# Streamed weight blocks on two DMA queues instead of one, with the small work of the loop moved to ScalarE

## The chip, the cores and the metric

The kernel runs on one core of one Trainium2 chip. The metric is the device time of one execution in microseconds (us), from the first instruction to the last. Below, "PE" is TensorE, "ACT" ScalarE, "DVE" VectorE, "POOL" GpSimd and "SP" SyncE, as the profile has them.

## The reference, cut to what matters

The output holds two independent computations side by side: a recurrent attention (A) and a long convolution (B). The change touches the loop of A only. It goes through 64 segments of 32 new tokens, and each segment needs the memory that the one before produced, so that segments cannot overlap freely:

```python
for s in range(n_seg):                               # 64 segments
    h = concatenate([mem, xs], axis=1)               # 8 memory rows + 32 rows of x
    q, k, v = h @ Wq, h @ Wk, h @ Wv                 # each 1024 x 4096, bf16
    p = softmax(where(mask, q @ k.T * scale, -1e9))
    o = (p @ v) @ Wo                                 # 4096 x 1024
    mem = o[:, :M, :]                                # feeds the next segment
    outs.append(o[:, M:, :])
```

The four matrices have 32 MB, 64 blocks of 512 KB. The kernel keeps 46 of them resident and streams the other 18 from HBM again in every segment.

## The kernel before

Eighteen blocks a segment are streamed, into a pool of four buffers. `unit` hands out a block and starts its load; PE reads the block in the order of the program.

```python
STREAM = {("k", 0): (0, 4), ("q", 0): (0, 4), ("k", 1): (0, 4), ("q", 1): (0, 4), ("v", 0): (0, 4), ("v", 1): (0, 4)}
STREAM_O = (0, 3, 5, 8, 11, 13)                      # 12 + 6 = 18 streamed blocks
...
    wst = ctx_w.enter_context(tc.tile_pool(name="a_wst", bufs=4, side="right"))
...
    def unit(key):
        if key in W_res:
            return W_res[key]                        # a resident block
        t_ = wst.tile([128, 2048], BF16, name="wst", tag="w")
        nc.sync.dma_start(out=t_[:], in_=WD[key][:])
        return t_
...
    # quads (projections): each block is read by 4 matmuls of 128x512
            for kc in kcs:
                w = unit((m, t, kc))
                for g in range(4):
                    nc.tensor.matmul(a[32 * g:32 * g + 32, :], lhsT=hT[:, kc, :], rhs=w[:, 512 * g:512 * g + 512], ...)
...
    # oproj (output projection): each block is read by 8 matmuls of 128x256
            for u in us:
                w = unit(("o", u))
                ...
```

The small loads (`pk`, `xt`), the small copies (`put_xt`, `new_kt`) and the five stores at the end of a segment are GpSimd's. In the change below they are the lines with a minus.

Of the kernel before, what the change touches and what calls it, by code (L numbers as in the profile page):

```python
# [175 lines left out]
def part_a(ctx, tc, x, mem0, src, WD, HE, seg_len, out_a, ahead, W_res, rest):  # L176
    nc = tc.nc
    S, Dm = x.shape
    M = mem0.shape[0]
    SL = seg_len  # L180
# [4 lines left out]
    XM = 24  # L185
    XL = SL - XM
    NK = SL + M
# [3 lines left out]
    XTd, PKd, OLd = ahead.XTd, ahead.PKd, ahead.OLd  # L191
# [16 lines left out]
    for g in range(4):  # L208
        p = slice(32 * g, 32 * g + 32)
# [8 lines left out]
    nc.gpsimd.affine_select(out=BDL[:], in_=BDL[:], compare_op=ALU.is_ge, fill=0.0, base=0, pattern=[[-8, 4], [-32, 4]], channel_multiplier=1)  # L218
    nc.gpsimd.affine_select(out=BDL[:], in_=BDL[:], compare_op=ALU.is_ge, fill=0.0, base=7, pattern=[[8, 4], [32, 4]], channel_multiplier=-1)

    def unit(key):
        if key in W_res:
            return W_res[key]
        t_ = wst.tile([128, 2048], BF16, name="wst", tag="w")
        nc.sync.dma_start(out=t_[:], in_=WD[key][:])
        return t_

    hT = const.tile([128, KC, SL], BF16, name="hT")
# [15 lines left out]

    def load_pk(j):
        pk = pers.tile([128, 768], BF16, name="pk", tag="pk")
        nc.gpsimd.dma_start(out=pk[:], in_=PKd[j])
        return pk

    def load_xt(j):  # L250
        xt = work.tile([128, KC, XM], BF16, name="xt", tag="F")
        nc.gpsimd.dma_start(out=xt[:].rearrange("p k r -> p (k r)"), in_=XTd[j])  # L252
        return xt

    def put_xt(xt):
        nc.gpsimd.tensor_copy(out=hT[:, :, 0:XM], in_=xt[:])

    def bc(ap, shape):
        return ap.to_broadcast(shape)

    put_xt(load_xt(0))
    pk = load_pk(0)
    for s in range(NS):
        vl = pk[:, 512:768].rearrange("p (t e) -> p t e", t=2)
        kl, ql = ([pk[:, 256 * t + o:256 * t + o + 128].rearrange("p (a g k) -> p a g k", a=4, g=4) for t in range(2)] for o in (0, 128))

        def quads(m, t, kcs, a=None):
            if a is None:
                a = ps_acc.tile([128, 512], F32, name="acc", tag="acc")
# [3 lines that stand above are left out]
                    nc.tensor.matmul(a[32 * g:32 * g + 32, :], lhsT=hT[:, kc, :], rhs=w[:, 512 * g:512 * g + 512],  # L273
                                     start=(kc == 0), stop=(kc == KC - 1), tile_position=(0, 32 * g), skip_group_check=True)
            return a
# [13 lines left out]

        def new_kt(t):  # L290
            k = work.tile([128, 4, 4, NK], BF16, name="KT", tag="C")
            nc.gpsimd.tensor_copy(out=k[:, :, :, SL:NK], in_=kl[t])  # L292
            return k

        def scores(t, QT, KT):
# [43 lines left out]
        def pv(p, t, V, pb, lbs, first=True):  # L339
            for hl in range(4):  # L340
                nc.tensor.matmul(p[:, hl, :], lhsT=V[:, 128 * hl:128 * hl + 128], rhs=pb[:, hl, :],
                                 start=(first and hl == 0), stop=False, skip_group_check=True)
            n = 4 // len(lbs)
            for i, lb in enumerate(lbs):
                nc.tensor.matmul(p[:, n * i:n * i + n, :].rearrange("p a b -> p (a b)"), lhsT=vl[:, t, :], rhs=lb,  # L345
                                 start=False, stop=True, skip_group_check=True)
# [9 lines left out]
        def evac_o(p, tag):  # L356
            o = work.tile([128, 4, 4, SL], BF16, name="oT", tag=tag)
            nc.scalar.copy(out=o[:], in_=p[:].rearrange("p a (g q) -> p a g q", g=4))  # L358
            return o

        def pv_l(pl_, t, V, L):

            pv(pl_[:, t], t, V, L[:, 0].rearrange("p (a b) k -> p a (b k)", a=4), [L[:, 1].rearrange("p a k -> p (a k)")], first=(t == 0))

        def oproj(po, us, oT):
            for u in us:
                w = unit(("o", u))
                for hh in range(2):
                    h = 2 * u + hh
                    for qt in range(4):  # L370
                        nc.tensor.matmul(po[32 * qt:32 * qt + 32, :], lhsT=oT[:, h % 4, (h % 16) // 4, :],  # L371
                                         rhs=w[:, 1024 * hh + 256 * qt:1024 * hh + 256 * qt + 256],
                                         start=False, stop=(h == 31), tile_position=(0, 32 * qt), skip_group_check=True)
# [4 lines left out]
        a = quads("k", 0, range(KC))  # L378
        k0 = evac(a, "A")
        KT0 = new_kt(0)  # L380
        a = quads("q", 0, range(KC))
        q0 = evac(a, "B")
# [9 lines left out]
        a = quads("q", 1, range(KC))  # L392
        q1 = evac(a, "B")
        KT1 = new_kt(1)
        p1 = new_tr()
        tr(p1, 0, k1, KT1[:, :, :, 0:SL])
# [18 lines left out]
        pp = ps_o.tile([128, 2, 256], F32, name="pp", tag="pp")  # L415
# [3 lines left out]
        if s + 1 < NS:  # L419
            xt = load_xt(s + 1)  # L420
        quads("v", 1, H1, a)
        V1 = evac(a, "E")
        if s + 1 < NS:
            put_xt(xt)
# [7 lines left out]
        pv1 = pv_x(1, V1, pk[:, 0:512].rearrange("p (a b) -> p a b", a=4), [lb1[:].rearrange("p a k -> p (a k)")], "B")  # L432
        o1 = evac_o(pv1, "B")
        pv_l(pl_, 1, V1, L1)
        if s + 1 < NS:
            pk = load_pk(s + 1)
        oproj(pp[:, 1, :], range(8, 16), o1)
        ob = work.tile([128, 2, 256], BF16, name="ob", tag="E")
        osb = ob[:, 0, :]
        nc.vector.tensor_copy(out=osb, in_=pp[:, 1, :])  # L440
        nc.scalar.copy(out=ob[:, 1, :], in_=pp[:, 0, :])
        if s + 1 < NS:
# [1 line left out]
            for j in range(2):  # L444
                nc.tensor.transpose(out=pt_o[:, j, :, :].rearrange("p a b -> p (a b)"), in_=osb[:, 128 * j:128 * j + 128], identity=ident[:])
            nc.vector.tensor_copy(out=hT[:, :, XM:SL].rearrange("p (q j) r -> p j q r", j=2), in_=pt_o[:, :, :, XM:SL])
        nc.gpsimd.dma_start(out=OLd[s], in_=ob[:, 1, :])
        r0 = s * SL
        for qt in range(4):
            nc.gpsimd.dma_start(out=out_a[r0:r0 + XM, 256 * qt:256 * qt + 256], in_=osb[32 * qt:32 * qt + XM, :])  # L450
    ctx_w.close()


    with tc.tile_pool(name="a_eo", bufs=1) as eo, tc.tile_pool(name="a_ew", bufs=16) as ew, \
# [3 lines left out]
        for u in range(16):  # L458
            if u in (0, 2, 4, 6):
# [3 lines left out]
                for n in range(2):  # L463
                    (nc.vector.tensor_copy if n == 0 else nc.scalar.copy)(
                        out=ol[b][:, 16 * n:16 * n + 16, :, :], in_=raw[:, :, 16 * n:16 * n + 16, :].rearrange("p s h k -> p h s k"))
# [13 lines left out]
        for b in range(4):  # L479
            ob = ex_.tile([128, Dm], BF16, name="oel", tag="oel")  # L480
# [586 lines left out]
def kernel(  # L1067
# [42 lines left out]
    with ExitStack() as ctx_a:  # L1110
        part_a(ctx_a, tc, A_x[0], A_mem0[0], src, WD, A_Wo.shape[0] * A_Wo.shape[1], seg_len, out_a, ahead, W_res, rest)
# [35 lines left out]
```

## Time and profile before

| what | before | from |
|---|---|---|
| median time | 2945.86 us (3 runs, 2942.58 to 2952.67) | timed runs |
| loop (first `ob` to last `ob`) | 1026.5 to 2842.2 us, 28.82 us a segment | line of `ob<-pp` |
| moved in the loop | 342 GB/s | busy time by stretch |
| PE waits for streamed blocks | 359 us | tile view |

### The profile page before, as it was taken

The page shows a single profiled execution, that of the slowest core. Times are in us where ns is not written, and L with a number is a line of the kernel's source. Part 1 is how long each engine was busy: PE and PEld are TensorE (multiplying, and loading weights), DVE is VectorE, ACT ScalarE, POOL GpSimd, SP SyncE. Part 2 cuts the span into 40 slices and gives each one's busy share as a digit, 9 for nine tenths or more (in the row PEclk, how much of TensorE's full clock was granted, in tenths as well). Part 3 has the DMA queues.
Part 4 walks back from the last instruction along what each step waited for, and adds up shares of the span by engine and source line. Part 5 has one row for each costly group of instructions (what it writes and reads, how often), then busy time and mean ns, then how long its engine had stood idle before and what let it go on. Part 6 is the DMA issues. An engine that isn't in the chain of part 4 may idle for free.

```text
span 2949.0 us, 75939 instructions
## 1 busy us (share of the span) xinstructions
PE 2124.8 (72%) x32791; PEld 1128.5 (38%) x32838; DVE 1355.8 (46%) x2622; ACT 967.4 (33%) x1394; POOL 599.2 (20%) x993
## 2 busy tenths in 40 slices
PE   1478777846887478777777777777777777777747
PEld 0246444622333244333343333333443333334323
DVE  7577677748983143434333333434333333434320
ACT  4767688731222122222222222222222222222210
POOL 2254435460001111111111111111111111111100
PEclk8689899968899798999899989999899899999978
DMA  4555654534338899999999999999999999999991
GB/s 113 155 156 154 183 164 119 150 115 125 112 128 291 327 348 335 343 338 350 333 352 337 343 332 345 350 345 348 329 336 343 324 353 331 352 339 348 348 322 49
DMA packets 376225, 800.93 MB, mean 272 GB/s; under 512 B 114678, under 2 KB 185334, under 8 KB 373840
## 3 DMA queue, kind: packets, MB, share of 16 engines
q1 hardware_dynamic: 335202, 722.51, 70.8%
q0 software_dynamic: 24912, 51.52, 5.2%
q10 hardware_dynamic: 15774, 22.03, 2.3%
q8 instruction: 257, 4.21, 0.6%
q14 instruction: 80, 0.66, 0.1%
HBM read 742.15 MB, written 67.37 MB: 275 GB/s over the span
## 4 chain that ended last, share of the span: by engine, by line
DMA 43%; PE 20%; issue 20%; DVE 6%; ACT 6%; POOL 5%; SPq 0%; ACTq 0%; POOLq 0%; DVEq 0%
DMA wst<-WD_o 14%; DMA wst<-WD_v 9%; PE acc L273 9%; DMA wst<-WD_k 8%; DMA wst<-WD_q 7%; PE pp L371 2%; PE pe L476 2%; DMA olr<-OLd 1%; ACT sn L859 1%; PE pro L125 1%; POOL us L743 1%; POOL us L744 1%; ACT oT L358 1%; PE tr L284 1%; PE ups L738 1%
## 5 line engine op out<-in xcount | busy, mean ns | idle before, releaser
L273 PEld LDWEIGHTS <-hT 128*32 128x32 bf16 x12288 | 320.7, 100 | 540.1 <-issue 256.7
L273 PE MATMUL acc<-wst,hT 128*32 128x512 bf16 x3072 | 330.2, 415 | 203.2 <-DMA wst<-WD_k 85.2
L279 ACT CAST ev<-acc 128x512 bf16<-128x512 f32 x384 | 225.4, 587 | 528.5 <-PE acc L273 485.8
L371 PEld LDWEIGHTS <-oT 128*32 128x32 bf16 x8192 | 227.8, 102 | 303.3 <-issue 209.8
L371 PE MATMUL pp<-wst,oT 128*32 128x256 bf16 x3072 | 167.0, 296 | 215.8 <-DMA wst<-WD_o 180.7
L285 DVE COPY KT<-tr 128x512 bf16<-128x512 bf16 x128 | 54.4, 425 | 539.8 <-PE tr L284 539.8
L273 PE MATMUL acc<-W_k,hT 128*32 128x512 bf16 x3072 | 249.7, 434 | 0.0
L371 PE MATMUL pp<-W_o,oT 128*32 128x256 bf16 x5120 | 231.5, 294 | 0.0
L273 PE MATMUL acc<-W_q,hT 128*32 128x512 bf16 x3072 | 224.8, 396 | 0.0
L273 PE MATMUL acc<-W_v,hT 128*32 128x512 bf16 x3072 | 212.7, 381 | 0.0
L440 DVE CAST ob<-pp 128x256 bf16<-128x256 f32 x64 | 27.2, 425 | 369.7 <-issue 365.2
L358 ACT CAST oT<-pv 128x512 bf16<-128x512 f32 x128 | 75.3, 588 | 255.7 <-PE pv L345 252.1
L311 DVE TENSOR_REDUCE mx<-sc 128x8 f32<-128x320 f32 x128 | 62.4, 487 | 197.7 <-PE sc L304 197.6
L1033 PE MATMUL yp<-Bt,mi 128*128 128x512 bf16 x379 | 113.8, 405 | 32.3 <-DVE Bt L987 16.3
L951 PE MATMUL hps<-KT,MF 128*128 128x512 bf16 x374 | 100.8, 415 | 49.4 <-DVE x L962 26.1
L252 POOL DMA_DIRECT2D xt<-XTd x64 | 35.9, 561 | 483.9 <-PE pp L345 395.8
L285 ACT COPY QT<-tr 128x512 bf16<-128x512 bf16 x128 | 75.0, 586 | 179.2 <-PE tr L284 141.6
L292 POOL COPY KT<-pk 128x128 bf16<-128x128 bf16 x128 | 38.4, 300 | 462.3 <-PE sc L304 449.4
L450 POOL DMA_DIRECT2D out_dram<-ob x256 | 129.7, 513 | 6.0 <-issue 5.9
L125 PE MATMUL pro<-xTl,wsl 128*128 128x512 bf16 x492 | 113.5, 380 | 8.4 <-DVE ua L740 4.6
L313 ACT ACTIVATE sc<-sc 128x320 f32<-128x320 f32 x128 | 54.0, 422 | 189.0 <-DVE sc L312 157.0
L835 DVE SCALAR_TENSOR_TENSOR nr<-kM,ptt 128x656 f32<-128x656 f32 x128 | 106.1, 829 | 21.5 <-ACT kM L834 18.2
(264 smaller groups left out, 3793.4 us busy)
## 6 DMA issues: line engine op xcount, KB each, us to landing
wst<-WD_o SPq DMA_DIRECT2D x384, 512.0 KB, 5.7
wst<-WD_k SPq DMA_DIRECT2D x256, 512.0 KB, 5.6
wst<-WD_q SPq DMA_DIRECT2D x256, 512.0 KB, 5.3
wst<-WD_v SPq DMA_DIRECT2D x256, 512.0 KB, 5.5
Ud<-ux POOLq DMA_DIRECT2D x16, 1024.0 KB, 5.7
uq<-Ud SPq DMA_DIRECT2D x32, 512.0 KB, 5.5
pk<-PKd POOLq DMA_DIRECT2D x64, 192.0 KB, 5.3
wsl<-in_A_Wk_dram SPq DMA_DIRECT2D x16, 512.0 KB, 4.2
```

Source lines behind the costliest of these rows:

```text
L125: nc.tensor.matmul(a[:], lhsT=w[:, kc, 128 * j:128 * j + 128], rhs=xTl[:, kc, :, :].rearrange("p s k -> p (s k)"), start=(kc == 0), stop=( ...
L273: nc.tensor.matmul(a[32 * g:32 * g + 32, :], lhsT=hT[:, kc, :], rhs=w[:, 512 * g:512 * g + 512], start=(kc == 0), stop=(kc == KC - 1), til ...
L279: nc.scalar.copy(out=q[:], in_=a[:])
L285: eng(out=dst, in_=p[:, i, :, :, :])
L311: nc.vector.tensor_reduce(out=mx[:], in_=sc, axis=AX.X, op=ALU.max)
L358: nc.scalar.copy(out=o[:], in_=p[:].rearrange("p a (g q) -> p a g q", g=4))
L371: nc.tensor.matmul(po[32 * qt:32 * qt + 32, :], lhsT=oT[:, h % 4, (h % 16) // 4, :], rhs=w[:, 1024 * hh + 256 * qt:1024 * hh + 256 * qt + ...
L450: nc.gpsimd.dma_start(out=out_a[r0:r0 + XM, 256 * qt:256 * qt + 256], in_=osb[32 * qt:32 * qt + XM, :])
L476: nc.tensor.matmul(pe[b][n][:], lhsT=ol[b][:, hi, :, :].rearrange("p s k -> p (s k)"), rhs=wos[u][:, 1024 * hh + 512 * n:1024 * hh + 512 * ...
L835: v.scalar_tensor_tensor(out=nrs[e // 4][:, e % 4].rearrange("p f t j -> p f (t j)"), in0=kM[:], scalar=MAGIC, in1=ptv, op0=ALU.subtract, ...
L951: pe.matmul(ps[:], lhsT=MF[:, 4 * rr + mc, cs, 128 * kc:128 * kc + 128], rhs=rhs, start=(i == 0 and mc == 0), stop=(i == 1 and mc == 3))
L1033: pe.matmul(yp[:], lhsT=m_[:, cs, kc, :], rhs=Bt[:, kc, half, j, c_, :], start=(n == 0), stop=(n == 15))
```

## The change

Its intent is to let two DMA queues feed the buffers by turns, so that neither queue has to issue every block. To keep other work from holding up the blocks that GpSimd issues (in the last experiment, where it does, they are issued 5.55 us after their buffer is free), all else that it did in the loop goes to ScalarE.

```diff
+    queues = [nc.gpsimd, nc.sync]
+
     def unit(key):
         if key in W_res:
             return W_res[key]
         t_ = wst.tile([128, 2048], BF16, name="wst", tag="w")
-        nc.sync.dma_start(out=t_[:], in_=WD[key][:])
+        queues.reverse()
+        queues[0].dma_start(out=t_[:], in_=WD[key][:])
         return t_
@@ load_pk, load_xt, put_xt, new_kt
-        nc.gpsimd.dma_start(out=pk[:], in_=PKd[j])
+        nc.scalar.dma_start(out=pk[:], in_=PKd[j])
-        nc.gpsimd.dma_start(out=xt[:].rearrange("p k r -> p (k r)"), in_=XTd[j])
+        nc.scalar.dma_start(out=xt[:].rearrange("p k r -> p (k r)"), in_=XTd[j])
-        nc.gpsimd.tensor_copy(out=hT[:, :, 0:XM], in_=xt[:])
+        nc.scalar.copy(out=hT[:, :, 0:XM], in_=xt[:])
-            nc.gpsimd.tensor_copy(out=k[:, :, :, SL:NK], in_=kl[t])
+            nc.scalar.copy(out=k[:, :, :, SL:NK], in_=kl[t])
@@ end of a segment
+        oproj(pp[:, 1, :], range(8, 16), o1)
         if s + 1 < NS:
             pk = load_pk(s + 1)
-        oproj(pp[:, 1, :], range(8, 16), o1)
...
-        nc.gpsimd.dma_start(out=OLd[s], in_=ob[:, 1, :])
+        nc.scalar.dma_start(out=OLd[s], in_=ob[:, 1, :])
...
-            nc.gpsimd.dma_start(out=out_a[r0:r0 + XM, 256 * qt:256 * qt + 256], in_=osb[32 * qt:32 * qt + XM, :])
+            nc.scalar.dma_start(out=out_a[r0:r0 + XM, 256 * qt:256 * qt + 256], in_=osb[32 * qt:32 * qt + XM, :])
```

## The prediction

> **What bounds the kernel now.** I read the page first, then the tile view of the streamed blocks, then the chain of waits inside two segments, then busy time by stretch.
>
> The page's slices say where the time is. From slice 13 on (about 990 us) the DMA row stands at 8 or 9 tenths without a break, while PE stands at 7:
>
> ```profile
> PE   1478777846887478777777777777777777777747
> DMA  4555654534338899999999999999999999999991
> GB/s 113 155 156 154 183 164 119 150 115 125 112 128 291 327 348 335 343 338 350 333 352 337 343 332 345 350 345 348 329 336 343 324 353 331 352 339 348 348 322 49
> q1 hardware_dynamic: 335202, 722.51, 70.8%
> q0 software_dynamic: 24912, 51.52, 5.2%
> DMA 43%; PE 20%; issue 20%; DVE 6%; ACT 6%; POOL 5%; SPq 0%; ACTq 0%; POOLq 0%; DVEq 0%
> ```
>
> Queue q1 is SyncE's, q0 GpSimd's, and the last line says that 43% of the chain that ended last is DMA; the page's next line names the four kinds of streamed block for 38 of these 43. This is the loop over 64 segments. Its length comes from the view of the line that ends a segment:
>
> ```profile
> L440 DVE CAST ob<-pp x64: 424/425/426, 1026.5 to 2842.2; 128x256 bf16<-128x256 f32 x64
> ```
>
> 63 periods in 1815.7 us, so 28.82 us each. A segment streams 18 blocks of 512 KB: 1.60 us per block. With pk, xt, the OLd store and four output stores (192 + 48 + 64 + 48 KB) it moves 9.80 MB, which makes 340 GB/s.
>
> The tile view shows who stands still for it:
>
> ```profile
> L225 SPq DMA_DIRECT2D wst<-WD_o x384: 319/320/1482, 1012.7 to 2835.3; - x192
> its engine sat idle before it (us, times) until:
>   DMA wst<-WD_o: 180.7, 231
>   DMA wst<-WD_k: 85.2, 81
>   DMA wst<-WD_q: 48.7, 109
>   DMA wst<-WD_v: 44.2, 62
> DMA to landing us min/median/max: 4.3/5.6/10.6
> ```
>
> The issue itself takes SyncE 0.32 us of each 1.60, so its sequencer is not the limit. PE waits 359 us for blocks, and a block lands 5.6 us after its issue. The chain of waits (1500 to 1560 us) shows the shape of one turn:
>
> ```profile
> 1501.64 5.97 DMA wst<-WD_o
> 1507.61 0.04 issue
> 1507.65 0.43 PE pp L371 x8
> 1508.08 0.02 issue
> 1508.09 5.92 DMA wst<-WD_o
> ```
>
> A buffer is read by PE (0.43), refilled (5.9), read again: 6.4 us a turn. Four buffers share the turns, and 6.4 / 4 is the 1.60 us per block. So the question is whether 5.9 us is work of the DMA engines or latency. The windows answer (microseconds; busy times; last three columns: granted clock, DMA share, GB/s):
>
> ```profile
> 925.00:940.00 15.00, 12.35 (x56) 5.24 (x56) 2.46 (x6) 4.87 (x8) 1.63 (x3) 1.00 1.04 400
> 984.00:1000.00 16.00, 0.00 (x0) 0.00 (x0) 0.00 (x0) 0.00 (x0) 0.00 (x0) 0.50 1.04 390
> 1500.00:2000.00 500.00, 382.88 (x7406) 197.66 (x7402) 188.09 (x481) 122.11 (x227) 79.52 (x172) 0.93 0.96 342
> ```
>
> From 984 to 1000 us SyncE's queue alone, with many blocks behind each other, moves 390 GB/s; from 925 to 940 us three queues together move 400. The loop runs at 342 / 395 = 87% of that. Mostly queueing, then, with a seventh left that the four buffers are not enough to fill.
>
> [...] The packet records of this trace[...]: on a quiet queue the first packet follows the issue by 1.01 us for SyncE (uq<-Ud), but 1.17 (Ud<-ux) and 1.97 (MId<-ms) for GpSimd, and 1.96 for pk in the loop.[...]
>
> **The change part by part.**
>
> (a) Streamed blocks. The blocks alternate, nine a segment on each queue. As both 18 and 4 are even, two buffers always belong to SyncE and two to GpSimd. Four are in flight as before; bytes and rows are the same. What is removed: 9 × 0.32 = 2.9 us of SyncE issue per segment, worth nothing since SyncE is 80% idle. What is added: GpSimd's start. I take 0.4 us more per GpSimd block, between the 0.16 (1.17 − 1.01) and the 0.96 (1.97 − 1.01) of the quiet queues. On half the blocks this is 0.2 us a turn on average, 0.2 / 6.4 = 3.1% of 1816 us: 57 us if all of it went through. [...]I let half through: **+28 us**.
>
> (b) Landing in pairs. [...]PE then reads two at once and the second's buffer stays idle for the first's 0.4 us of reading. If this happens for one pair in four, 0.1 us a turn on half the buffers, and half through: 0.05 / 6.4 × 1816 / 2, **+7 us**.
>
> (c) Small copies. The 128x128 copy takes GpSimd 300 ns[...]; hT<-xt (192 columns) 349[...]. The two K copies stand behind k and q evacuations with idle time of 1 us and more after them: nothing. The xt copy is different: [...]the copy stands between V1's and o1's evacuation and waits for the xt load, which is issued at o0's. In the trace o1 starts a mean 0.52 us after xt has landed; in 33% of the segments the landing plus 0.35 us of copy is later than o1's start, a mean push of 0.21 us over all. 63 × 0.21 = 13 us; PE often waits for the next o block there anyway, so half: **+7 us**.
>
> (d) Stores. GpSimd issues five stores at 0.51 to 0.55 us each; ScalarE's sequencer takes 0.33 to 0.44 for a load of this trace and does it beside its own arithmetic. So the last store leaves about 0.7 us sooner. QT<-tr shares its buffer with ob, and waits for these stores 7 times, 18.2 us in all:
>
> ```profile
>   DMA out_dram<-ob: 18.2, 7
> ```
>
> I credit two thirds: **−12 us**. The stores' 1.8 us on ScalarE fall into the gap before k's evacuation (3.7 us in the segment at 1515 us).
>
> (e) Semaphores. [...]a block can wait for an earlier small DMA. I followed each wait of one segment to its producer: k0 waits for the last store of the segment before, v1's for OLd, q1's for pk. All are several microseconds old by then. **0.**
>
> (f) The later place of the pk load changes nothing: ScalarE has no work between its two places.
>
> Sum: 28 + 7 + 7 − 12 = +30 us: 2946 + 30, about **2975 us**.
>
> **The rivals.**
>
> *The second queue fills the idle seventh.* If one queue stalls between blocks and two cover for each other, the loop could reach 395 GB/s: 9.80 MB / 395 = 24.8 us a segment, 64 × 4.0 = 256 us less, about 2690. For it: 400 GB/s with three queues, and 22 ns of excess in the mean 4 KB packet (181 ns in the loop, median 159), as if something held engines up. Against it: one queue did 390 without any help once enough was queued, and the number in flight stays at four. I hold a tenth of this possible.
>
> *GpSimd's latency goes through whole.* Both parities of buffer are read in order, so the slower pair sets the pace. With 0.8 us on each turn of GpSimd's buffers, 0.8 / 6.4 = 12% of the loop, or +227 us: 3170. For it: the chain above returns to the same buffer, so a GpSimd turn would close on itself. Against it: the 5.9 us are mostly other blocks' packets[...]. A quarter of it through would already be 3000.
>
> *Nothing visible.* The engines are the bound, queues are names, the small moves cancel: 2946 ± 15.
>
> **Range and chances.** The low end, 2915, is a first rival with a tenth of its gain plus the stores; the high end, 3060, is half of the second. Slower by over 2% means above 3005: the sum would have to double, which a start of 0.8 us instead of 0.4 does. I give that 0.30. Faster by over 2% (below 2887) needs a cause that I only see as packet excess: 0.07. Within 2%: 0.63.
>
> **What would show it.** Step (a): segment period from 28.8 to about 29.3 us, GB/s from 342 to about 336; GpSimd's blocks land later than SyncE's. If both land alike at 5.6, (a) is wrong. A DMA share above 0.96 with 350 GB/s or more would be the first rival. (c): "ACT hT<-xt" idle until the xt load, and o1 pushed; more PE wait for oT than the 32.5 us now. (d): the line of out_dram<-ob gone from QT's waits. The prediction fails if the two queues' blocks land so unevenly that PE waits far longer than 359 us, or if ScalarE's wait for xt proves to gate the second half of the output projection in every segment.

Cut passages are marked: they said of the hardware what no trace or run here shows. No term of the sum is cut, 28 + 7 + 7 − 12 = +30 us. That two queues make blocks land in pairs (b), and that half of a delay goes through (a, b), were assumptions and not shown by a trace at the time.

## More of the kernel before

One line is to be compared later and is not in the prediction: busy time in a stretch of the loop. Its columns are the stretch and its length, then busy us (and instructions) of PE, PE's weight loads, DVE, ACT and POOL, then PE's granted clock, the DMA engines' busy share and GB/s.

```profile
1300.00:2800.00 1500.00, 1145.25 (x22120) 591.55 (x22112) 549.29 (x1404) 362.75 (x677) 240.52 (x520) 0.93 0.96 342
```

## The result, and the profile after

The changed kernel takes 3132.3 us (median of 4 runs, 3127.32 to 3150.22), against 2949.27 (4 runs, 2942.58 to 2959.34) for the kernel before. The ratio is 1.063, with a 95% interval of 1.058 to 1.068: 183 us slower, and outside the predicted range. Here and below a ratio is the mean time of one kernel's runs over that of the kernel before in the same rounds, so it is not quite the ratio of the medians.

The page of the changed kernel, the rows that answer to those of before (granted clock, DMA share and GB/s in 40 slices; then the queues; then the chain):

```profile
PEclk7699989878987888898988889898898898889878
DMA  4456643453368988898988999898989898989881
GB/s 118 135 156 187 189 137 106 124 160 104 121 216 311 320 300 300 311 316 299 320 295 301 314 321 337 309 320 298 336 314 310 310 331 294 313 313 321 304 314 54
...
q1 hardware_dynamic: 252258, 420.48, 39.6%
q0 software_dynamic: 91472, 330.44, 31.0%
q10 hardware_dynamic: 52638, 45.13, 4.7%
...
DMA 36%; PE 25%; issue 23%; DVE 6%; ACT 5%; POOL 4%; SPq 1%; ACTq 0%; POOLq 0%; DVEq 0%
```

The bytes are where they were meant to go: q0 (GpSimd) has 330 MB instead of 52, q10 (ScalarE) the small ones. But the row of GB/s fell from some 340 to some 310, and the DMA row now has 8s where it was nearly all 9s. In the chain, the DMA share fell while PE and "issue" rose: a wait for a block ends the step less often, and PE with blocks at hand is on the path more often. The stretch of the loop says the same in one line:

```profile
1300.00:2800.00 1500.00, 1094.69 (x20338) 560.87 (x20331) 506.07 (x1294) 368.65 (x766) 231.16 (x430) 0.88 0.90 314
```

The DMA engines are less busy (0.90 for 0.96) in a kernel that waits for them. The line that ends a segment gives the length of the loop:

```profile
L443 DVE CAST ob<-pp x64: 423/425/425, 1035.3 to 3021.8; 128x256 bf16<-128x256 f32 x64
```

That is 1986.5 us for 63 periods, 31.53 us each, 2.71 more than before. The loop took 171 us of the difference of the two profiled spans (3128.9 − 2949.0 = 180), the part before the loop 9. The issues of the largest kind of block, from the tile view:

```profile
L228 SPq DMA_DIRECT2D wst<-WD_o x192: 319/320/320, 1019.8 to 3012.4; - x192
L228 POOL DMA_DIRECT2D wst<-WD_o x192: 537/537/547, 1021.4 to 3013.5; - x192
```

That view also lists how long the engines sat idle before these instructions, but it now counts GpSimd's idle time before its own loads too. So PE's waits are taken from the view of waits (us in total, times, longest):

```profile
PE pp L374 <- DMA wst<-WD_o: 251.2, 194, 5.1
PE acc L276 <- DMA wst<-WD_k: 120.5, 56, 36.1
PE acc L276 <- DMA wst<-WD_q: 59.4, 56, 2.8
PE acc L276 <- DMA wst<-WD_v: 53.3, 53, 2.8
```

They sum to 484 us, 125 more than before, in 359 waits instead of 483: fewer and longer. PE's busy time grew as well, by 60 us (2124.8 to 2184.8), while its granted clock in the loop fell from 0.93 to 0.88; the two together are about the whole loss. Yet a block lands as soon after its issue as before. To see this, I followed each of 1044 blocks (segments 4 to 61) through the trace's records and cut the turn of its buffer into four terms: from the last matmul on the buffer's old block to the issue of the new one; from issue to landing (the last of the sixteen landing records that the trace has of each of these blocks); from landing to PE's first matmul on it; and PE's reading. Eighteen blocks pass through four buffers, so 4.5 turns make a segment. Means in us, worked out from the traces, not a view of the profile:

```
                free->issue  issue->landed  landed->use  reading   turn   x 4.5
before             0.043         5.625         0.316       0.431    6.42    28.9
after              0.191         5.631         0.752       0.451    7.03    31.6
difference        +0.148        +0.006        +0.436      +0.020
x 4.5 x 64 (us)      43             2           126           6      total 176
```

The four terms are the whole turn, so their sum has to come out near the loop's 171 us; it says where the time is lost and not why. Most of it, 126 us, is a term in which the block *has landed and waits*. Blocks that wait for PE, and a PE that waits longer for blocks, go together when blocks come unevenly. The time from one block's landing to the next one's in order shows it:

```
gap between landings (us)    10%    median   90%    below 1.0    0.14 to 0.24
before                       1.26    1.31    2.42   0 of 1044      0
after                        0.22    1.52    3.26   201 of 1044   95
```

With one queue the gap is hardly ever below 1.26 us (40 of 1044 are under 1.25, the least is 1.06). A block has 128 rows of 4 KB. At this trace's median of 159 ns a row, and spread evenly over the 16 engines of the page, they would take 128 × 159 / 16 ns = 1.27 us; this is an estimate, as the trace does not say which engine a row was on.

With two queues, 201 gaps are shorter than 1.0 us, and nearly half of those lie near 0.18 us, about one row. The rows of the two blocks of a pair are mostly not mixed, though. In these 95 pairs the eighth of the sixteen landing records of the one block and that of the next lie a mean 1.33 us apart, near the median gap of 1.31 us with one queue. And at the instants between 1300 and 2800 us at which 14 rows or more are under way, a mean 83% of them belong to one of the two queues (an estimate for comparison: 16 rows, each of either queue with equal chance, would give about 60%). What comes late is the end of a block: from its eighth landing record to its last, a block takes a mean 1.50 us here (1.65 on GpSimd's queue), 1.22 before. Why it comes late was not shown. The 201 blocks with a short gap wait a mean 1.58 us for PE, the other 843 a mean 0.56; so a little over half of the rise from 0.316 lies on these 201. In the changed kernel the two closest are a GpSimd block and the SyncE block that follows it: the median gap is 2.09 us from SyncE's to GpSimd's and 1.27 from GpSimd's to SyncE's, and 28% of the latter are below 0.5 us.

### The profile page after: what moved, and what is told of

Its sections match the earlier page's. It is cut to its first block, busy times and chain, and to the rows that moved or that the text cites. A ratio compares the mean times of both kernels' runs of the same rounds, so it can differ in the third digit from the quotient of the medians.

```text
span 3128.9 us, 75624 instructions
## 1 busy us (share of the span) xinstructions
PE 2184.8 (70%) x32791; PEld 1152.1 (37%) x32838; DVE 1355.3 (43%) x2622; ACT 1014.5 (32%) x1586; POOL 611.7 (20%) x929
## 4 chain that ended last, share of the span: by engine, by line
DMA 36%; PE 25%; issue 23%; DVE 6%; ACT 5%; POOL 4%; SPq 1%; ACTq 0%; POOLq 0%; DVEq 0%
PE acc L276 13%; DMA wst<-WD_o 11%; DMA wst<-WD_k 10%; DMA wst<-WD_v 6%; DMA wst<-WD_q 5%; PE pp L374 2%; PE pe L479 2%; ACT sn L862 1%; ACT oT L361 1%; PE pro L125 1%; PE tr L287 1%; POOL us L746 1%; POOL us L747 1%; DMA olr<-OLd 1%; PE ups L741 1%
## 5 line engine op out<-in xcount | busy, mean ns | idle before, releaser
L276 PEld LDWEIGHTS <-hT 128*32 128x32 bf16 x12288 | 333.1, 105 | 619.8 <-issue 388.0
L276 PE MATMUL acc<-wst,hT 128*32 128x512 bf16 x3072 | 348.8, 441 | 253.4 <-DMA wst<-WD_k 120.5
L374 PEld LDWEIGHTS <-oT 128*32 128x32 bf16 x8192 | 237.7, 105 | 367.1 <-issue 271.4
L276 PE MATMUL acc<-W_k,hT 128*32 128x512 bf16 x3072 | 273.5, 471 | 0.0
L276 PE MATMUL acc<-W_q,hT 128*32 128x512 bf16 x3072 | 248.1, 431 | 0.0
L228 POOL DMA_DIRECT2D wst<-WD_o x192 | 103.2, 538 | 510.9 <-PE acc L276 370.4
L228 POOL DMA_DIRECT2D wst<-WD_k x128 | 68.8, 538 | 508.8 <-PE acc L276 266.4
L228 POOL DMA_DIRECT2D wst<-WD_v x128 | 68.8, 538 | 394.3 <-PE acc L276 374.4
L444 ACT CAST ob<-pp 128x256 bf16<-128x256 f32 x64 | 23.8, 373 | 370.0 <-DVE ob L443 362.9
L228 POOL DMA_DIRECT2D wst<-WD_q x128 | 68.8, 538 | 319.5 <-PE pp L374 176.6
```

The source lines that it names most:

```text
L228: queues[0].dma_start(out=t_[:], in_=WD[key][:])
L374: nc.tensor.matmul(po[32 * qt:32 * qt + 32, :], lhsT=oT[:, h % 4, (h % 16) // 4, :], rhs=w[:, 1024 * hh + 256 * qt:1024 * hh + 256 * qt + ...
```

## The experiments

Theory 1: two queues make blocks land unevenly, often in pairs; as PE reads in order, a buffer then idles with a landed block, and fewer loads are in flight; a later start on one of the queues makes it worse. Rivals: GpSimd's queue is slow as such (theory 2 of the first expectations); the work moved to ScalarE costs the time (theory 3); the DMA engines or PE's clock do. The later expectations use the numbers anew and say what they mean.

All kernels gave correct results. The two with five buffers, the control with halves on one queue and the one with finer turns ran beside a kernel before of 2943.58 us, the other eight beside one of 2951.7.

### One queue, small work moved (SyncE)

The changed kernel with every block on SyncE, so that only the small moves are left:

```diff
-    queues = [nc.gpsimd, nc.sync]
+    queues = [nc.sync, nc.sync]
```

> The moves to ScalarE alone: all streamed blocks stay on SyncE's queue. Theory 1 (two queues let blocks land bunched, so a landed block waits for PE to finish its predecessor: 0.75 us from landing to use instead of 0.32) and theory 2 (GpSimd's own path is the cost: later issue, slower start) both expect the time of before, 2935 to 2965 us, with 0.3 us from landing to use. Theory 3 (the moves to ScalarE cost: ScalarE stands in order behind xt and the stores) expects 3020 or more.

Measured: 2998.85 us (2993.34 to 3011.25), ratio 1.016 [1.011, 1.021], between what theories 1 and 2 and what theory 3 expected. The 47 us are nearly all in free→issue: 0.20 us instead of 0.043, and +0.157 × 4.5 × 64 = 45. Landing to use is 0.295, no worse than before. The view of the waits of SyncE's queue (waiting line, what it waited for, us in total, times, longest) has a line that neither the kernel before nor the changed one has:

```profile
SPq L228 <- DMA OLd<-ob: 75.5, 63, 2.8
```

The data of a weight load give no reason to wait for a store of `OLd`, once a segment. In the traces of the kernel before and of the changed one, though, SyncE's and ScalarE's DMAs name the same eight semaphores (1533 and 69 DMAs before, 957 and 517 after), GpSimd's others. Here three blocks of a segment were issued 0.8 to 1.0 us after their buffer was free, each with the semaphore of a DMA still in flight.

### The same, with the stores back on GpSimd

```diff
     (on top of the kernel above)
-        nc.scalar.dma_start(out=OLd[s], in_=ob[:, 1, :])
+        nc.gpsimd.dma_start(out=OLd[s], in_=ob[:, 1, :])
-            nc.scalar.dma_start(out=out_a[...], in_=osb[...])
+            nc.gpsimd.dma_start(out=out_a[...], in_=osb[...])
```

> As the run with the small work alone on ScalarE, but the five stores of a segment stay on GpSimd[...]. If the 47 us of that run are waits for semaphores that ScalarE's stores share with SyncE's blocks, the blocks of k1 and q1 are issued 0.04 us after their buffer is free again, and the time is that of before, 2935 to 2965 us. If the copies or the xt load on ScalarE cost it, 2980 us or more remain.

Measured: 2947.3 us (2943.32 to 2949.8), ratio 0.9986 [0.9964, 1.0009]; free→issue is back at 0.045. The same view has no wait for a store any more:

```profile
SPq L228 <- DMA wst<-WD_o: 187.9, 262, 2.7
SPq L228 <- DMA wst<-WD_v: 169.8, 238, 2.8
SPq L228 <- DMA wst<-WD_k: 146.9, 201, 3.0
SPq L228 <- DMA wst<-WD_q: 126.6, 196, 2.0
```

So the loads and copies on ScalarE cost nothing, and the five stores cost 50 us *where SyncE issues all blocks*. In the changed kernel SyncE issues only half, and this wait does not occur: SyncE's own blocks are issued 0.043 us after their buffer is free. The small moves are not where its 183 us went.

### All blocks on GpSimd's queue

```diff
-    queues = [nc.gpsimd, nc.sync]
+    queues = [nc.gpsimd, nc.gpsimd]
```

> One queue again, but GpSimd's: all streamed blocks there, the rest on ScalarE. Theory 1 expects regular landings again (landing to use back to 0.3 to 0.4 us) and only GpSimd's later issue, 0.3 us on every 6.4 us turn, at most 4.7% of the loop: 2950 to 3035 us. Theory 2 expects every block to pay what half of them pay after the change: 3130 us or more, up to 3300.

Measured: 3036.27 us (3032.26 to 3038.72), ratio 1.028 [1.024, 1.032]. Issue to landing is 5.615 us, as on SyncE. GpSimd's queue is not slow; it only issues 0.348 us after a buffer is free where SyncE needs 0.043. Of these 0.305 us, 0.24 arrive in the turn (6.42 to 6.66): four fifths, 69 us. No gap is below 1.0 us. The time is 1 us above theory 1's range and far below theory 2's. A slow GpSimd queue is refuted as the main cause: with twice as many blocks on it, the kernel is 96 us faster than the changed one.

### Two hardware queues

The kernel before with its blocks by turns on ScalarE and SyncE, GpSimd keeping the small work. ScalarE has other work in the loop, so a load is put right behind the matmuls that free its buffer:

```diff
+    plan = [key for _ in range(NS) for key in streamed_keys()]
+    ahead_t = []
+    queues = [nc.scalar, nc.sync]
+    def fetch():
+        if plan:
+            t_ = wst.tile([128, 2048], BF16, name="wst", tag="w")
+            queues.reverse()
+            queues[0].dma_start(out=t_[:], in_=WD[plan.pop(0)][:])
+            ahead_t.append(t_)
+    for _ in range(4):
+        fetch()
     def unit(key):
-        ...                       # tile and load here
+        return W_res[key] if key in W_res else ahead_t.pop(0)
+    (fetch() after the matmuls of each streamed block)
```

> Blocks alternate between SyncE's and ScalarE's queue, GpSimd keeps the small work as before; each refill is written into the program right after the block whose buffer it takes, so that ScalarE does not hold it back. Theory 1 (two queues as such) expects the same bunching without GpSimd: landing to use 0.6 us or more, 3040 to 3100 us. Theory 2 expects the time of before, 2930 to 2970, with landing to use near 0.3.

Measured: 3009.28 us (3000.46 to 3016.26), ratio 1.018 [1.013, 1.023]. Both queues issue within 0.06 us, no GpSimd is involved, and still landing to use rises from 0.316 to 0.467 us; 124 of 1044 gaps are below 1.0. Two queues alone made pairs here. Both expectations missed: the effect is there, but smaller than theory 1 had it. Of the 58 us, 39 are in the turns, 1.3%; the loop also starts 17 us later here, which nothing explains.

### Two hardware queues, one late

Theory 1 splits here: 1a, blocks bunch because one queue answers sooner than the other; 1b, GpSimd's queue beside SyncE's bunches by itself. ScalarE's blocks now wait for a small copy into their buffer, which must itself wait for the buffer:

```diff
     (on top of the kernel above)
+            if queues[0] is nc.scalar:
+                nc.scalar.copy(out=t_[:, 0:64], in_=ident[:, 0:64])
             queues[0].dma_start(...)
```

> SyncE and ScalarE alternating, with ScalarE's issue made 0.3 us late by a small copy into the buffer ahead of it. Theory 1a expects what the change shows: landing to use 0.65 us or more, 3090 to 3160 us. Theory 1b expects landing to use near the 0.47 us of the two hardware queues, and only the delay, 0.15 us a turn on average: 3030 to 3060 us.

Measured: 3089.68 us (3084.86 to 3095.66), ratio 1.047 [1.044, 1.050]. ScalarE issues 0.403 us after a free buffer, SyncE 0.042. Landing to use rises to 0.63 us, and the gaps below 1.0 to 168. The figures lie just short of 1a's range and well above 1b's. This is three quarters of the change's loss without a block on GpSimd.

### Both queues equally late

The changed kernel, with SyncE made nearly as late as GpSimd by a one-element memset in front of its loads:

```diff
         queues.reverse()
+        if queues[0] is nc.sync:
+            nc.gpsimd.memset(t_[0:1, 0:1], 0.0)
         queues[0].dma_start(out=t_[:], in_=WD[key][:])
```

> The changed kernel with SyncE's issue made late as well: a one-element memset on GpSimd into the buffer must end before SyncE's block is issued, so both queues issue 0.3 us or more after PE has freed the buffer, where before only GpSimd's blocks did. Theory 1a (the bunching comes from one queue answering sooner than the other) expects landing to use to fall from 0.75 to 0.5 us or less, and the time to stay near the change's 3130 or fall below it although an issue delay was added. Theory 1b[...] expects landing to use to stay at 0.7 us or more and the added delay on top: 3160 us or more.

Measured: 3079.33 us (3071.17 to 3094.65), ratio 1.044 [1.039, 1.049]: 53 us *faster* than the changed kernel, though half of its loads start 0.22 us later (0.261 for 0.043; GpSimd 0.341). Gaps below 1.0 fall from 201 to 123, and landing to use from 0.752 to 0.531, near the 0.5 that 1a had set. (The memset also makes SyncE's loads wait for GpSimd's work in between, but the order of issue hardly changed by it: 5 of 1044 blocks were issued ahead of their predecessor in the changed kernel, and 2 here.) This is the strongest evidence that the loss is in the pattern of arrivals and not in latency. Put together, the kernels with two queues stand in nearly one order by pairs, by the time from a block's eighth landing record to its last, and by the time that landed blocks lie idle (means in us from the records, cut as above):

```
                free->issue  issue->landed  8th->16th  landed->use   gaps < 1.0   median us
one queue, SP      0.043         5.625         1.22       0.316       0 of 1044     2951.7
one queue, POOL    0.348         5.615         1.15       0.259       0             3036.3
two_hw             0.059         5.588         1.30       0.467     124             3009.3
late_sync          0.301         5.548         1.33       0.531     123             3079.3
late_scalar        0.223         5.564         1.44       0.630     168             3089.7
after              0.191         5.631         1.50       0.752     201             3132.3
```

### A fifth buffer, on the kernel before

The space comes from one resident block, so 19 blocks a segment are streamed:

```diff
-STREAM_O = (0, 3, 5, 8, 11, 13)
+STREAM_O = (0, 2, 4, 7, 9, 11, 13)
-    wst = ctx_w.enter_context(tc.tile_pool(name="a_wst", bufs=4, side="right"))
+    wst = ctx_w.enter_context(tc.tile_pool(name="a_wst", bufs=5, side="right"))
```

> The kernel before with five buffers for streamed blocks instead of four; their space is paid with one resident block, so 19 blocks a segment are streamed instead of 18. Theory 1 (the loop is limited by the turns of the buffers, about 6.4 us each, and not yet by the DMA engines): with one more block in flight the engines reach about 390 GB/s, 10.3 MB in 26.5 us a segment, and the time falls to 2780 to 2850 us in spite of the extra block. Theory 2 (the engines are the bound at 342 GB/s): one block more costs 1.5 us a segment, about 3040 us. Landing time under theory 2 would be 5.6 x 5/4 = 7.0 us or more; under theory 1 about 6.3 us.

Measured: 2854.39 us (2834.29 to 2859.95), ratio 0.968 [0.962, 0.974]. It beats both kernels, with more bytes:

```profile
1300.00:2800.00 1500.00, 1162.50 (x22635) 599.05 (x22627) 561.73 (x1436) 372.06 (x698) 245.98 (x532) 0.94 0.99 375
```

So the kernel before was limited by the turns of its four buffers, with the DMA engines not quite full. The time is 4 us above theory 1's range, and a block lands 6.2 us after its issue, as theory 1 had it. The median gap between landings is 1.28 us here, near the 1.27 us estimated above from the time of a row.

### A fifth buffer, on the changed kernel

The same two lines.

> The changed kernel with the same fifth buffer and 19 streamed blocks (with an odd number of buffers, blocks of both queues pass through every buffer). Theory 1 (uneven landings cost time because four buffers leave no slack for a block that has landed and waits for its predecessor to be read): with a fifth buffer much of the loss goes, and this kernel is at most 3% slower than the five-buffer form of the kernel before. Rival (the loss is in the engines or in PE's clock, whatever the buffers): it stays at about 6% against that form.

Measured: 3007.91 us (2998.76 to 3019.74), ratio 1.022 [1.017, 1.027]. Against the five-buffer form of the kernel before this is 1.0217 / 0.9683 = 1.055. A fifth buffer was to take much of the loss away, and it did not:

```profile
1300.00:2800.00 1500.00, 1139.48 (x21495) 585.74 (x21498) 529.29 (x1355) 384.82 (x808) 259.08 (x481) 0.89 0.96 350
```

The terms are the same as with four: against the one-queue form, free→issue rises by 0.148 us (0.043 to 0.191) and landing to use by 0.433 (0.436 to 0.869), and 276 of 1102 gaps are below 1.0. So a part of theory 1 fell: it is not a want of slack in four buffers that one more would cure. The 5.5% is near what the rival expected (about 6%). The engines are not quite full here either, at 0.96 for the 0.99 of the one-queue form; but PE's clock is 0.89 for 0.94, and this run does not part the clock from the arrivals.

### Each block as two halves on both queues, and its control

Every block as two loads of 64 partitions, to let both queues work on the same block:

```diff
-        queues.reverse()
-        queues[0].dma_start(out=t_[:], in_=WD[key][:])
+        nc.sync.dma_start(out=t_[0:64], in_=WD[key][0:64])
+        nc.gpsimd.dma_start(out=t_[64:128], in_=WD[key][64:128])
```

> Both queues, but each block is cut in two halves of 64 partitions, one on each queue, so that both queues carry the same block at a time[...]. Theory 1 expects landing to use back to about 0.3 us, GpSimd's later issue on every block: 2960 to 3035 us. Theory 2 expects every block to wait for GpSimd's half: 3130 us or more.

Measured: 3633.27 us (3619.0 to 3644.4), ratio 1.230 [1.224, 1.236]. The 4 KB rows took a median of some 270 ns instead of 159, so the experiment had changed more than was meant. The control has both halves on SyncE (`nc.sync` in both lines).

> Control of the run that cut each block into two 64-partition halves on two queues (3633 us): the same halves, both on SyncE's queue. If the halves themselves are slow (packets of 268 ns in that run against 159), this stays above 3500 us. If two queues running at once slowed the packets, this comes back to about 3000 us, with packets near 160 ns.

Measured: 4019.9 us (4004.0 to 4030.99), ratio 1.365 [1.359, 1.371], and rows of 291 ns on a single queue. The halves themselves are slow, and neither run can tell the theories on whole blocks apart. Between the two, though, the one with two queues is the faster, by 387 us. SyncE alone has two loads a block to issue and issues them a mean 1.7 and 2.3 us after the buffer is free; on two queues both halves are issued after 0.3. Here issuing was late, and the second queue helped.

### Finer turns

The kernel before with each block as two tiles of 1024 columns in eight half-size buffers, all on SyncE:

```diff
-    wst = ... bufs=4
+    wst = ... bufs=8
-        t_ = wst.tile([128, 2048], ...); nc.sync.dma_start(out=t_[:], in_=WD[key][:])
+        for i in range(2):
+            t_ = wst.tile([128, 1024], BF16, name="wst", tag="w")
+            nc.sync.dma_start(out=t_[:], in_=WD[key][:, 1024 * i:1024 * i + 1024])
```

> The kernel before with every block as two tiles of 1024 columns (256 KB, rows of 2 KB) in eight buffers of half the size, all on SyncE's queue. The same bytes, and the same space. If the turns of the buffers limit the loop, finer turns keep more in flight (a half comes free after half the reading) and the time falls to 2800 to 2900 us. If the engines' time per row eats the gain (87 ns for 2 KB against 159 for 4 KB, 9% more per byte), it stays at 2950 us or more.

Measured: 2954.54 us (2951.38 to 2956.15), ratio 1.003 [1.000, 1.007]: the second expectation. The engines are fuller without moving more:

```profile
1300.00:2800.00 1500.00, 1213.35 (x22076) 613.62 (x22080) 548.66 (x1404) 361.26 (x675) 240.27 (x520) 0.94 0.98 342
```

Rows of 2 KB take a mean of 93 ns, 186 for what a 4 KB row did in 181, and two issues a block raise free→issue to 0.26 us. Whether finer turns gain anything with rows of full size stays open.

### The alternation without the moves

The kernel before with only the two queues in `unit`; the small work stays on GpSimd.

```diff
-        nc.sync.dma_start(out=t_[:], in_=WD[key][:])
+        queues.reverse()
+        queues[0].dma_start(out=t_[:], in_=WD[key][:])
```

> The alternation alone, with all small work left on GpSimd, where blocks now stand in order behind copies that wait for PE and for xt. All theories expect it to be slower than the whole change, 3200 us or more, with GpSimd's blocks issued 1 us or more after their buffer is free; if it is not, moving the small work away was no need of the change.

Measured: 4324.74 us (4320.6 to 4333.86), ratio 1.466 [1.462, 1.470].

```profile
  DMA wst<-WD_o: 579.9, 129
  DMA wst<-WD_v: 445.1, 130
  DMA wst<-WD_k: 348.5, 64
...
  DMA wst<-WD_q: 235.0, 93
```

These sum to 1609 us; without GpSimd's own idle time, which this view counts too, PE waits 1431 us for blocks. GpSimd's loads stand in order behind copies and stores that wait for the attention, and are issued a mean 5.55 us after their buffer is free. So with the small work left on GpSimd, the alternation is far worse than the whole change.

## Why the prediction was wrong, point by point

**The bound** was read rightly: four buffers' turns of 6.4 us, with engines close to full. The fifth buffer confirmed it.

**(b) "Landing in pairs" is the step that failed.** It was named beforehand, and the end of a block does come later (1.50 us from the eighth landing record to the last, 1.22 before); but its term was put at +7 us and measured 126 as landing to use (some of which may be PE's slower clock, see below). All three of its factors were too small. Pairs: "one pair in four" on half the buffers, that is one gap in eight; 201 of 1044 are below 1.0 us, about one in five. Idle time: 0.4 us, the reading of the first block. But PE does not go from one streamed block to the next; resident blocks lie between them, and of the blocks that had landed before PE began on their predecessor (171), the median came to be read 1.55 us after that beginning. Passing through: "half"; no shorter queue took up any of it, as issue to landing stayed at 5.63 us. A term of 0.025 us a turn became 0.436. And (b) treated GpSimd's lag as a separate cost, while the runs show that a difference between the two queues makes more pairs: with SyncE nearly as late as GpSimd, there are 123 instead of 201, as with two hardware queues, and 53 us came back.

**(a) GpSimd's start** was assumed at 0.4 us more per block and is 0.296 (0.339 against 0.043), all of it ahead of the issue. The prediction took it from the quiet queues' first packets, behind the issue. (Its 1.01 us for SyncE holds for the loads before 770 us; three later ones on a quiet queue have 0.59.) Behind the issue, the loop shows next to nothing (issue to landing 5.66 us for GpSimd's blocks, 5.61 for SyncE's). "I let half through" failed: the run with all blocks on GpSimd passed four fifths on, and in the changed kernel the queue in front of a late block got no shorter. So 43 us in place of +28. The sign set for this step, landing alike at 5.6 us, was given as showing (a) wrong; it did, for the place of the lag, though not for its existence.

**(c) The small copies** cost less than +7. They take ScalarE as long as they took GpSimd (301 for 300 ns, `hT<-xt` 352 for 349). These are waits of the changed kernel after 1000 us:

```profile
ACT hT L259 <- DMA xt<-XTd: 166.3, 63, 4.5
...
PE pp L374 <- ACT oT L361: 34.0, 67, 1.2
```

ScalarE does wait for `xt` in all 63 segments, as feared, but `xt` lands 4.28 us after its issue (4.99 before), `o1` starts later than its matmuls allow in 7 segments, a mean 0.05 us over all instead of 0.21, and PE's wait for `oT` is 34.0 us against 32.5.

**(d) The stores.** In the trace before, 42 of ScalarE's 69 issues overlap an instruction of its own, as the prediction has it. The wait of QT for the stores did shrink, from 18.2 us to the 7.4 of the line below. But the prediction read too much into the 18.2: only 9.7 of them came after the transposes that QT needs (3.6 of the 7.4). Nor does the wait seem to reach the end: with the stores back on GpSimd it was 41.3 us, at the time of the kernel before.

```profile
ACT QT L288 <- DMA out_dram<-ob: 7.4, 3, 3.7
```

**(e) Semaphores: 0** was right for the changed kernel and would have been wrong by 47 us for its one-queue form, where I had not looked.

**(f)** shows nothing, as predicted; no run isolated it.

**The rivals.** The second queue filled no idle seventh: 314 GB/s is less than 342. (The low end of the range, a tenth of this rival's 256 us and the stores' 12, adds up to 2908 and not to 2915.) The second rival, 3170, came nearest in time, but for a reason that it did not have: of its latency of 0.8 us nothing is to be seen. The sentence on what would make the prediction fail, blocks that land "so unevenly that PE waits far longer than 359 us", describes what came: 484 us.

**What stays open.** The late ScalarE queue is later than GpSimd (0.403 for 0.339 us) and yet makes fewer pairs; some 43 us between that kernel and the changed one have no shown cause, and GpSimd's own queue may hold it. How much of landing to use comes from PE's slower clock, no run separated: matmuls on resident blocks took 59 us more (918.7 to 977.8, summed over the four lines of the two pages), so it may be a part of the 126 but hardly most of it. The clock may follow from the waiting, which is not shown either: in the control with halves, where rows are slow on a single queue, it was 0.73 in the same stretch. Why the end of a block comes late is open too.

## What to carry to other kernels

If a few buffers are filled in a fixed order and read in the same order, keep the loads on one queue: here it delivered them one after the other (no gap below 1.0 us among 1044 blocks), while on two queues the end of one block often came together with the next (124 such gaps), and a late one of the two made this worse (168 and 201). Before splitting a stream, ask whether issuing is the limit (here SyncE was four fifths idle) and what order the reader needs. One more buffer on the one queue, at the price of one more block to stream, gave 3.2%, where the second queue took 6.3%.
